# D times x: from TensorE's diagonal products to GpSimd and the eviction

## The chip, the cores and the metric

The kernel runs on one core of a Trainium2 chip. The time is the device time of one execution in microseconds (us); the time before is the median of three runs. The profile comes from one further execution.

## The reference

A state-space block and an attention block work on the same x (2048 rows, 1024 columns) and are mixed by a gate for each row.

```python
g = sigmoid((x * gate_w).sum(-1, keepdims=True))
# state space: h_t = Lam_bar * h_{t-1} + B_bar x_t, complex, 1024 states
y = 2.0 * einsum("blp,dp->bld", hseq, Cmat).real + x * Dskip
# attention: 32 heads of 32, softmax(q k / sqrt(32)) v, times wo
out = g * y + (1 - g) * b
```

All inputs and the output are bf16. The change is about the term `x * Dskip` in y: it adds, in each column, x times a number of that column.

## The kernel before

**Bursts set the beat.** Attention is cut into 512 bursts. Each has eight matmuls of scores (line 1624), two exponentials on ScalarE (ACT) from PSUM into bf16 tiles (lines 1643 and 1640, 1024 or 768 elements a partition) and products of earlier exponentials with V (line 1709) on TensorE (PE). Where an exponential has only 768 elements, the other 256 are done by VectorE (DVE) as a polynomial: line 1633 takes them from PSUM (the exponential of the same bank waits for it), lines 1667, 1668 and 1664 work on them, and GpSimd (POOL) writes the last step, x_p, in line 1665; line 1688 multiplies them with V on TensorE.

**Dense chains fill the rest.** The builder goes through the bursts one by one, calls each a period (number p, and pg = p mod 64 within one of eight head groups g), and gives each about four matmuls of 512 columns of a dense chain. All dense chains use PSUM bank 7, one after the other, and VectorE evicts the bank at the end of a chain. There are these chains: Q, K and V of the next head group (lines 1426 and 1445), u = B x (line 1457, 64 chains of eight matmuls), C chains (line 1504, 32 of them) and output chains (line 1535). An instruction's place on each engine's queue is its place in the builder's order; waits are on semaphores and worked out by `Sched`.

**State space.** A chunk of 512 rows and 128 states is an item: its u is stored to DRAM, loaded again in one piece (line 1474), rotated, scanned and rotated back on VectorE (lines 1353 and 1362). `item_ops` puts this work in a list, and the builder gives VectorE as much of it in each period as its own cost constants let it. Four chunks follow each other; GpSimd copies the last column of each (line 1365) and works out the next start (`carry`).

**A C chain** is `d_c`: 128 rows and 512 columns of y, 16 matmuls over states and real and imaginary part. Four diagonal products are put among them, each 128 by 128, with x as stationary operand and a diagonal matrix of D as moving one (lines 1508 to 1511). GpSimd builds the eight diagonals in the opening (`diag_d`, line 1306). The eviction (line 1517) multiplies by the gate into the fp32 tile Ag, of which there is one, and a DMA from SyncE's queue (SP, line 1518) stores it to DRAM; output chains load it again late in the kernel.

**Loads.** Q's weights have one slot, K's and V's two each, by head group. The builder loads K's and V's for group g + 2 at pg = 25 and Q's for g + 1 at pg = 28 (lines 1832 to 1838); Q's chains may begin at pg 32 or later, K's at any time in the group before, and all are forced when the rest of the group only just holds them. The matrix C is loaded by transposing DMAs, two for each of eight column blocks, one block every four periods from p = 28 (`C_LOADS`), and folded on VectorE afterwards. Output weights take over the places of weights that are no longer needed (`wo3`).

Of the kernel before, what the change touches and what calls it, by code (L numbers as in the profile page):

```python
# [922 lines left out]
GROUPS = 8  # L923
# [35 lines left out]
class FastPath:  # L959

    def __init__(self, nc, S, es, d, flag):
# [11 lines left out]
        wb = T("wb", [128, 8192], BF)  # L973
        self.wq = wb[:, 0:1024].rearrange("p (a n) -> p a n", a=8)
        self.wkv = wb[:, 1024:5120].rearrange("p (s q a n) -> p s q a n", s=2, q=2, a=8)
        self.bT = wb[:, 5120:8192].rearrange("p (s a n) -> p s a n", s=3, a=8)

        row = lambda o, n: wb[:, o:o + 1024 * n].rearrange("p (a n) -> p a n", a=n)
        self.wo3 = [row(1024, 2), row(5120, 3), row(3072, 1), self.cT[0][:, 0:1, :], self.cT[0][:, 1:2, :]]
        self.wo = [(self.wo3[0][:, a, :], "wo0") for a in range(2)] + [(self.wo3[4][:, 0, :], "wo4")] + [(self.wo3[1][:, a, :], "wo1") for a in range(3)]  # L980
# [6 lines left out]
        self.hpx = wb[:, 5120:8192].rearrange("p (k n) -> p k n", k=6)  # L987
# [15 lines left out]
        self.gcol = T("gcol", [128, 2, 16], F32)  # L1003
        self.ident = T("ident", [128, 128], BF)
        self.ones = self.xp[:, 0:128]
        self.diagD = T("diagD", [128, 8, 128], BF)
        self.init = T("init", [128, 2, 8], F32)
        self.hl = T("hl", [128, 2, 8], F32)
        self.cm = T("cm", [128, 4, 8], F32)
# [53 lines left out]
                     [], [("xr", r + k) for k in range(n // 128)], "ld_x", eng)  # L1063

    def w_of(self, g, part):
        return (self.wkv[:, g % 2, part - 1], ("w", g % 2, part)) if part else (self.wq, ("w", 0, 0))

    def ld_w(self, g, part, eng="sp"):
        cb = 1024 * part + 128 * g
# [83 lines left out]
    def opening(self):  # L1153
# [10 lines left out]
        for word in self.OPENING.split():  # L1164
# [9 lines left out]
            elif op in ("Ka", "Qa"):  # L1174
                self.half256(int(op == "Ka"), i, 0)
            elif op == "Kb":
                self.half256(1, i, 1)
                evac(self.K[:, 0, 256 * i:256 * (i + 1)], 7, ("K", 0, i // 2), i % 2 == 0)
            elif op == "Qb":
                self.half256(0, i, 1)  # L1180
                evac(self.Q[:, i // 2, 256 * (i % 2):256 * (i % 2 + 1)], 7, ("Q", i // 2), i % 2 == 0)
                self.spare(0.5)
            elif op in ("Va", "Vb"):
                bank, h, kt = 6, int(op == "Vb"), 2 * i + int(op == "Vb")

# [12 lines left out]
            elif op == "G":  # L1198
                g = self.gcol
                self.act(lambda e: e.activation(g[:, 0, :], g[:, 0, :], ACT.Exp, scale=-1.0), [("g0", i) for i in range(8)], ["g0"])  # L1200
                dve(lambda e: e.tensor_scalar(g[:, 0, :], g[:, 0, :], 1.0, None, ALU.add), ["g0"], ["g0"])
                dve(lambda e: e.reciprocal(g[:, 0, :], g[:, 0, :]), ["g0"], ["g0"])
                dve(lambda e: e.tensor_scalar(g[:, 1, :], g[:, 0, :], -1.0, 1.0, ALU.mult, ALU.add), ["g0"], ["g1"])
            elif op == "B":
                self.burst(8 * U + i)()
                while self.later and self.later[0][0] <= self.p:
                    self.later.pop(0)[1]()
                self.p += 1
            elif op == "M":
                S.op("pe", lambda e: e.matmul(ps[:, 6, 0:40], self.prow, self.ident[0:40, 0:40], start=True, stop=True),  # L1210
                     reads=[("prm", i) for i in range(5)] + ["ident", ("ht", 0)], writes=[("bank", 6)], name="prm")
                dve(lambda e: e.tensor_copy(self.pf[:, 0:5, :], ps[:, 6, 0:40].rearrange("p (a b) -> p a b", a=5)), [("bank", 6)],
                    [("pf", i) for i in range(5)], "prm")
# [3 lines left out]
                self.diag_d()  # L1217

    def spare(self, us):
        while self.nmath and us > 0:  # L1220
# [80 lines left out]
        ts(B2, P(FR), -2.0, ALU.mult, q(FR))  # L1301
        return ops

    def diag_d(self):
        for j in range(8):
            self.pool(lambda e, j=j: e.tensor_scalar(self.diagD[:, j, :], self.ident[:], self.pf[:, 3, j:j + 1], 0.0, ALU.mult, ALU.add),
                      ["ident", ("pf", 3)], [("diagD", j)])

    def fold_ops(self, j):

# [185 lines left out]
    def d_c(self, ch, tq, cb, k):  # L1496
# [8 lines left out]
                            tok[:1] + [("cTf", ri, j, cb)]))  # L1505


        for q in range(4):
            dt = 4 * cb + q
            mms.insert(5 * q + 3, (0, lambda e, f, l, q=q, dt=dt: e.matmul(ps[:, 7, 128 * q:128 * (q + 1)], xT[:, dt, 128 * tt:128 * (tt + 1)], self.diagD[:, dt, :],  # L1510
                                                                          start=False, stop=False), [("diagD", dt)] + self.xtok(ch)))
        a = self.Ag
        at = "Ag"
        tile = 2 * tt + cb

        def evac():
            self.dve(lambda e: e.tensor_scalar(a, ps[:, 7, :], self.gcol[:, 0, tt:tt + 1], None, ALU.mult), [("bank", 7), "g0"], [at], "evac_c")
            self.dma(lambda e: e.dma_start(self.agd[tile], a), [at], [("agd", tile)], "st_a")
            self.c_left[ch] -= 1
            self.c_end = self.p  # L1520
        return self.chain(mms, "c", evac)

    def ld_a(self, k):

# [209 lines left out]
    def build(self):  # L1734
# [7 lines left out]
        self.begin()  # L1742
        for m in range(3):
            self.ld_b(m)
        for part in (1, 2):
            self.ld_w(1, part)
        self.plan()
        self.pt_own = {}
        self.x_of, self.x_batch, self.x_when = {}, [], {}
# [40 lines left out]
        for p in range(first, NBURST):  # L1790
# [40 lines left out]

            if pg == 25 and g + 2 < GROUPS:
                assert g or not (proj[0] or cur and cur.tag == "proj")
                for part in (1, 2):
                    self.ld_w(g + 2, part)
            if pg == 28 and g + 1 < GROUPS:
                assert not (cur and cur.tag == "proj")
                self.ld_w(g + 1, 0)
            wsv = self.d["B_wo"].rearrange("(a p) n -> p a n", p=128)
            if p == 386:  # L1840
                self.dma(lambda e: e.dma_start(self.wo3[0], wsv[:, 0:2, :]), [], ["wo0"] + [("w", 0, q) for q in (1, 2)], "ld_wo")
            if not cs and cur is None and not wo1 and self.c_left[3] == 0:
                wo1 = True
                self.dma(lambda e: e.dma_start(self.wo3[1], wsv[:, 3:6, :]), [], ["wo1"] + [("bT", r) for r in range(3)] + [("hp", 8, k) for k in range(6)], "ld_wo")
            if g >= 6 and not wo6 and not cs and self.c_left[3] == 0:
                wo6 = True
                self.dma(lambda e: e.dma_start(self.wo3[3], wsv[:, 6:7, :]), [], ["wo3", ("cT", 0, 0), ("cTf", 0, 0, 0), ("cTf", 0, 0, 1)], "ld_wo")
                self.dma(lambda e: e.dma_start(self.wo3[4], wsv[:, 2:3, :]), [], ["wo4", ("cT", 0, 1), ("cTf", 0, 1, 0), ("cTf", 0, 1, 1)], "ld_wo")
            if g >= 6 and not last and not proj[7] and not us and not cs and cur is None and not self.bg:

                last = True
                xs = [("xr", r) for r in range(16)]
                assert wo1 and wo6
                self.dma(lambda e: e.dma_start(self.wo3[2], wsv[:, 7:8, :]), [], ["wo2"] + [("w", 1, q) for q in (1, 2)] + xs, "ld_wo")
# [6 lines left out]
            while used < quota:  # L1861
                if cur is None:
# [4 lines left out]
                    elif not last:  # L1867
# [268 lines left out]
```

## Time and profile before

| what | us |
|---|---|
| median of the three runs | 928.48 (926.41 to 932.98) |
| profiled execution, its own time | 928.11 |
| its span in the profile | 926.3 |
| ACT busy | 907.3 |
| TensorE busy | 902.5 |
| VectorE busy | 758.4 |
| GpSimd busy | 86.8 |

Busy time of TensorE is modelled and counts overlapping matmuls once; a busy ACT or TensorE may still be the one that waits for the other, so the page alone does not tell which of the two sets the pace. In rows of the timeline stand start, length, engine, line, operation, output and inputs, count, and in brackets the idle time before with what ended it. `SPq` marks DMA instructions in SyncE's queue.

### The profile page before, as it was taken

What the parts mean: (1) busy time and instruction counts of PE and PEld (TensorE: products, weight loads), DVE (VectorE), ACT (ScalarE), POOL (GpSimd) and SP (SyncE); (2) the same over time, 40 slices, a digit from 0 to 9 for tenths busy, and PEclk for the clock granted to TensorE, in tenths of its full rate; (3) what the DMA queues carried; (4) which work ended last, traced back from release to release, by engine and by line L of the source; (5) the groups of instructions that cost most, each with busy time, mean ns of one, the idle gap of its engine ahead of it and who ended that gap; (6) DMA issues with size and microseconds to landing.
All of it is one profiled execution on the core that took longest, in us unless ns stands there. A gap on an engine that the chain in (4) does not pass through costs nothing.

```text
span 926.3 us, 33979 instructions
## 1 busy us (share of the span) xinstructions
PE 902.5 (97%) x15316; PEld 503.9 (54%) x15316; DVE 758.4 (82%) x1310; ACT 907.3 (98%) x1034; POOL 86.8 (9%) x156
## 2 busy tenths in 40 slices
PE   8899999999999999999999999999999999999996
PEld 4554754557555565546655565555655655445553
DVE  2788989998989999989989999899988655776665
ACT  6999999999999999999999999999999999999996
POOL 2000000111000101011111020000010010001010
PEclk9999999999999999999999999999999999999998
DMA  9569747750457101272012511413001112424312
GB/s 195 87 116 184 93 84 138 144 116 5 81 113 152 50 20 49 67 147 53 19 51 65 126 45 31 104 63 103 20 15 43 31 51 77 156 83 128 114 62 75
DMA packets 170934, 77.69 MB, mean 84 GB/s; under 512 B 147232, under 2 KB 155424, under 8 KB 170784
## 3 DMA queue, kind: packets, MB, share of 16 engines
q1 hardware_dynamic: 168624, 74.94, 36.3%
q8 instruction: 121, 1.98, 0.9%
q10 hardware_dynamic: 2160, 0.53, 0.3%
q14 instruction: 29, 0.24, 0.1%
HBM read 25.18 MB, written 20.97 MB: 50 GB/s over the span
## 4 chain that ended last, share of the span: by engine, by line
PE 52%; ACT 40%; DVE 4%; DMA 2%; SPq 1%; issue 1%; POOL 0%; DVEq 0%; ACTq 0%
ACT f_pt L1643 32%; PE f_ps L1709 14%; PE f_ps L1624 10%; PE f_ps L1426 9%; PE f_ps L1504 7%; PE f_ps L1457 6%; ACT f_pt L1640 5%; PE f_ps L1445 5%; SPq L1062 1%; ACT f_cT L1643 1%; PE f_ps L1688 1%; DMA f_xT<-in_A_x_dram 1%; ACT f_Et L1643 1%; DMA f_wb<-in_A_B_im_dram 1%; DMA f_ub<-u_scratch 0%
## 5 line engine op out<-in xcount | busy, mean ns | idle before, releaser
L1643 ACT ACTIVATE f_pt<-f_ps 128x1024 bf16<-128x1024 f32 x760 | 728.8, 1090 | 1.5 <-PE f_ps L1624 1.3
L1709 PEld LDWEIGHTS f_ps<-f_V,f_pt 128*128 128x128 bf16 x7184 | 222.2, 96 | 95.3 <-issue 68.7
L1709 PE MATMUL f_ps<-f_V,f_pt 128*128 128x33 bf16 x7184 | 258.0, 178 | 0.0
L1624 PE MATMUL f_ps<-f_Q,f_K 32*128 32x256 bf16 x4096 | 203.3, 273 | 10.8 <-ACT f_pt L1643 3.3
L1640 ACT ACTIVATE f_pt<-f_ps 128x768 bf16<-128x768 f32 x184 | 165.3, 898 | 0.7 <-PE f_ps L1624 0.6
L1624 PEld LDWEIGHTS f_ps<-f_Q,f_K 32*128 32x128 bf16 x4096 | 60.7, 92 | 148.0 <-ACT f_pt L1643 120.6
L1457 PE MATMUL f_ps<-f_xT,f_wb 128*128 128x512 bf16 x512 | 131.5, 379 | 1.6 <-DMA f_wb<-in_A_B_im_dram 0.7
L1665 POOL TENSOR_SCALAR f_xp<-f_xq 128x512 int16<-128x512 f32 x92 | 67.3, 732 | 646.0 <-DVE f_xq L1664 471.3
L1426 PE MATMUL f_ps<-f_xT,f_wb 128*128 128x512 bf16 x464 | 119.3, 379 | 0.1
L1633 DVE TENSOR_SCALAR f_xi<-f_ps 128x256 int32<-128x256 f32 x184 | 77.4, 421 | 17.6 <-PE f_ps L1624 13.3
L1362 DVE TENSOR_TENSOR_SCAN f_ht<-f_pf,f_init,f_ut 128x512 bf16<-128x512 f32 x64 | 81.3, 1279 | 0.0
L1504 PE MATMUL f_ps<-f_cT,f_hp 128*128 128x512 bf16 x272 | 74.5, 379 | 0.1
L1667 DVE SCALAR_TENSOR_TENSOR f_xq<-f_xi 128x512 f32<-128x512 uint16 x92 | 63.7, 692 | 3.2
L1668 DVE SCALAR_TENSOR_TENSOR f_xq<-f_xq,f_xi 128x512 f32<-128x512 f32 x92 | 63.6, 692 | 3.1
L1664 DVE SCALAR_TENSOR_TENSOR f_xq<-f_xi,f_xq 128x512 f32<-128x512 int16 x92 | 63.5, 690 | 2.6
L1457 PEld LDWEIGHTS f_ps<-f_xT,f_wb 128*128 128x128 bf16 x512 | 40.1, 96 | 40.5 <-issue 8.6
L1535 PE MATMUL f_ps<-f_wb,f_OT 128*128 128x512 bf16 x188 | 61.2, 381 | 0.4 <-DVE f_Et L1547 0.4
L1445 PE MATMUL f_ps<-f_wb,f_xT 128*128 128x128 bf16 x896 | 59.3, 219 | 0.0
L1426 PEld LDWEIGHTS f_ps<-f_xT,f_wb 128*128 128x128 bf16 x464 | 36.1, 96 | 35.6 <-issue 7.6
L1461 DVE CAST f_ub<-f_ps 128x512 bf16<-128x512 f32 x64 | 44.1, 688 | 10.4 <-PE f_ps L1457 9.7
L1445 PEld LDWEIGHTS f_ps<-f_wb,f_xT 128*128 128x128 bf16 x896 | 50.4, 97 | 3.8 <-issue 3.8
L1722 DVE RECIPROCAL f_rc<-f_ps 128x8 f32<-128x8 f32 x63 | 13.1, 207 | 47.6 <-PE f_ps L1688 43.5
(149 smaller groups left out, 822.5 us busy)
## 6 DMA issues: line engine op xcount, KB each, us to landing
u_scratch<-f_ub SPq DMA_DIRECT2D x64, 128.0 KB, 2.1
f_ub<-u_scratch SPq DMA_DIRECT2D x32, 256.0 KB, 3.0
ag_scratch<-f_Ag SPq DMA_DIRECT2D x32, 256.0 KB, 2.0
f_hp<-ag_scratch SPq DMA_DIRECT2D x32, 256.0 KB, 3.0
f_wb<-in_B_wqkv_dram SPq DMA_DIRECT2D x21, 256.0 KB, 4.1
out_dram<-f_xT SPq DMA_DIRECT2D x16, 256.0 KB, 2.2
f_OT<-f_On SPq DMA_TRANSPOSE x63, 2.3
f_wb<-in_B_wo_dram SPq DMA_DIRECT2D x1, 768.0 KB
```

Of the source, the lines that this page charges most:

```text
L1362: ops.append((1.24, lambda ri=ri: dve(lambda e: e.tensor_tensor_scan(ht[:, ri, :], rr, ut[:, ri, :], self.init[:, ri, j:j + 1], ALU.mult, ...
L1426: mms.append((1, lambda e, f, l, a=a, w=w: e.matmul(ps[:, bank, :], w[:, a, :], xT[:, a, 512 * ch:512 * (ch + 1)], start=f, stop=l), [tok] ...
L1445: m = e.matmul(ps[:, bank, 128 * q:128 * (q + 1)], xT[:, a, 128 * kt:128 * (kt + 1)], w[:, a, :], start=(a == 0), stop=(a == 7))
L1457: mms.append((1, lambda e, f, l, a=a: e.matmul(ps[:, 7, :], bT[:, (2 * n + ri) % 3, a, :], xT[:, a, 512 * ch:512 * (ch + 1)], start=f, sto ...
L1504: mms.append((1, lambda e, f, l, j=j, ri=ri, h=h: e.matmul(ps[:, 7, :], h[:, cols], cT[ri][:, j, 512 * cb:512 * (cb + 1)], start=f, stop=l ...
L1624: m = e.matmul(ps[:, 2 * sl[h // 2] + h % 2, 256 * kl:256 * (kl + 1)], K[32 * h:32 * h + 32, g % 2, 128 * kt:128 * (kt + 1)], Q[32 * h:32 ...
L1633: first = self.dve(lambda e: e.tensor_scalar(self.xi[:, b % 2, X_COLS * n:X_COLS * (n + 1)], ps[:, 2 * s + 1, 512 - X_COLS:512], X_A, X_LO ...
L1640: self.S.op("act", lambda e: e.activation(flat(self.tile[p]), flat(ps[:, 2 * s:2 * s + 2, :]), ACT.Exp, scale=SCALE), reads=[("S", s)], wr ...
L1643: self.act(lambda e: e.activation(self.tile[p], ps[:, 2 * s:2 * s + 2, :], ACT.Exp, scale=SCALE), [("S", s)], [("pt", p)], "exp")
L1665: self.pool(lambda e: e.tensor_scalar(bits, xq[:], X_K, 128.0 * (E0 + 126.0), ALU.mult, ALU.add), ["xq"], p2, "x_p")
L1667: return [(0.73, 0.0, lambda: self.dve(lambda e: e.scalar_tensor_tensor(xq[:], lo, E2 / E3 * w, lo, ALU.add, ALU.mult), i2, ["xq"], "x_q") ...
L1709: m = e.matmul(ps[:, 6, o:o + 33], self.tile[p][:, h2, 256 * kl + 128 * qt:256 * kl + 128 * (qt + 1)], V[:, g % 2, 2 * i + kl, h, :], star ...
```

## The change

The diagonals, their tile and the four products a chain go. D is loaded as a row, broadcast to all partitions (`Dbc`), and for each C chain the matching 128 by 512 tile of x is loaded as it is stored (`xn`). When a C chain starts, GpSimd multiplies the two into Ag and scales Ag by the gate; the eviction becomes one instruction, bank times gate plus Ag. There is one `xn`; the load for the next C chain is issued two periods after a chain starts.

```diff
-        self.diagD = T("diagD", [128, 8, 128], BF)
+        self.Dbc = T("Dbc", [128, 1024], BF)
+        self.xn = T("xn", [128, 512], BF)
...
+    def ld_skip(self, tile):
+        tt, cb = divmod(tile, 2)
+        self.dma(lambda e: e.dma_start(self.xn[:], self.x2[128 * tt:128 * (tt + 1), 512 * cb:512 * (cb + 1)]), [], ["xn"], "ld_xn")
+
+    def skip(self, tile):
+        tt, cb = divmod(tile, 2)
+        self.pool(lambda e: e.tensor_tensor(self.Ag, self.xn[:], self.Dbc[:, 512 * cb:512 * (cb + 1)], ALU.mult), ["xn", "Dbc"], ["Ag"], "skip")
+        self.pool(lambda e: e.tensor_scalar(self.Ag, self.Ag, self.gcol[:, 0, tt:tt + 1], 0.0, ALU.mult, ALU.add), ["g0"], ["Ag"], "skip")
...
-            self.dve(lambda e: e.tensor_scalar(a, ps[:, 7, :], self.gcol[:, 0, tt:tt + 1], None, ALU.mult), [("bank", 7), "g0"], [at], "evac_c")
+            self.dve(lambda e: e.scalar_tensor_tensor(a, ps[:, 7, :], self.gcol[:, 0, tt:tt + 1], a, ALU.mult, ALU.add), [("bank", 7), "g0"], [at], "evac_c")
...
+            if p == C_LOADS + 34:
+                self.dma(lambda e: e.dma_start(self.Dbc[:], self.d["A_Dskip"].unsqueeze(0).to_broadcast([128, 1024])), [], ["Dbc"], "ld_D")
+                self.ld_skip(cs[0][1].tile)
...
                             cur = cs.pop(0)[1]
+                            self.skip(cur.tile)
+                            if cs:
+                                self.later.append((p + 2, lambda t=cs[0][1].tile: self.ld_skip(t)))
```

The loads move. `C_LOADS` becomes 36. K's weights have one slot instead of two and are loaded at pg = 0 of the group before theirs (for group 1 at period 17, no longer in the opening), Q's at pg = 38; V's stay. K's chains may begin at pg = 4, Q's at pg = 42.

```diff
-C_LOADS = 28
+C_LOADS = 36
+W_AT = (38, 0, 17)
...
-                proj[g][8 + c].after = max(16 * c, 32)
+                proj[g][c].after = W_AT[1] + 4
+                proj[g][8 + c].after = max(16 * c, W_AT[0] + 4)
...
-                for part in (1, 2):
-                    self.ld_w(g + 2, part)
-            if pg == 28 and g + 1 < GROUPS:
-                assert not (cur and cur.tag == "proj")
+                self.ld_w(g + 2, 2)
+            if pg == W_AT[1 if g else 2] and g + 1 < GROUPS:
+                self.ld_w(g + 1, 1)
+            if pg == W_AT[0] and g + 1 < GROUPS:
+                assert not proj[0]
                 self.ld_w(g + 1, 0)
```

The weight tile shrinks by 1024 columns, and the output weights' rows are laid out anew: row 1 moves from the weight tile, where it was loaded at period 386, to a place in C's tile beside row 2, loaded after the last C chain.

More of the change, by code (lines that the diff above doesn't have):

```diff
@@ L972, in __init__ @@
         self.V = T("V", [128, 2, 16, 4, 33], BF)
[L973 to L976, printed above, removed]
+        wb = T("wb", [128, 7168], BF)
+        self.wq, self.wk = (wb[:, 1024 * k:1024 * (k + 1)].rearrange("p (a n) -> p a n", a=8) for k in range(2))
+        self.wv = wb[:, 2048:4096].rearrange("p (s a n) -> p s a n", s=2, a=8)
+        self.bT = wb[:, 4096:7168].rearrange("p (s a n) -> p s a n", s=3, a=8)
         row = lambda o, n: wb[:, o:o + 1024 * n].rearrange("p (a n) -> p a n", a=n)
-        self.wo3 = [row(1024, 2), row(5120, 3), row(3072, 1), self.cT[0][:, 0:1, :], self.cT[0][:, 1:2, :]]
-        self.wo = [(self.wo3[0][:, a, :], "wo0") for a in range(2)] + [(self.wo3[4][:, 0, :], "wo4")] + [(self.wo3[1][:, a, :], "wo1") for a in range(3)]
+        self.wo3 = [row(2048, 1), row(4096, 3), row(3072, 1), self.cT[0][:, 0:1, :], self.cT[0][:, 1:3, :]]
+        self.wo = [(self.wo3[0][:, 0, :], "wo0")] + [(self.wo3[4][:, a, :], "wo4") for a in range(2)] + [(self.wo3[1][:, a, :], "wo1") for a in range(3)]
         self.wo += [(self.wo3[3][:, 0, :], "wo3"), (self.wo3[2][:, 0, :], "wo2")]
@@ L1065, in w_of @@
     def w_of(self, g, part):
-        return (self.wkv[:, g % 2, part - 1], ("w", g % 2, part)) if part else (self.wq, ("w", 0, 0))
+        return [(self.wq, ("w", 0, 0)), (self.wk, ("w", 0, 1)), (self.wv[:, g % 2], ("w", g % 2, 2))][part]
     def ld_w(self, g, part, eng="sp"):
@@ L1302, in math @@
         return ops
[L1304 to L1307, printed above, removed]
+    def ld_skip(self, tile):
[5 more added lines that the diff above has]
+        self.pool(lambda e: e.tensor_scalar(self.Ag, self.Ag, self.gcol[:, 0, tt:tt + 1], 0.0, ALU.mult, ALU.add), ["g0"], ["Ag"], "skip")
     def fold_ops(self, j):
@@ L1505, in d_c @@
                             tok[:1] + [("cTf", ri, j, cb)]))
[L1508 to L1511, printed above, removed]
         a = self.Ag
@@ L1520, in evac @@
             self.c_end = self.p
-        return self.chain(mms, "c", evac)
+        dn = self.chain(mms, "c", evac)
+        dn.tile = tile
+        return dn
     def ld_a(self, k):
@@ L1744, in build @@
             self.ld_b(m)
-        for part in (1, 2):
-            self.ld_w(1, part)
+        self.ld_w(1, 2)
         self.plan()
@@ L1840, in build @@
             if p == 386:
-                self.dma(lambda e: e.dma_start(self.wo3[0], wsv[:, 0:2, :]), [], ["wo0"] + [("w", 0, q) for q in (1, 2)], "ld_wo")
+                self.dma(lambda e: e.dma_start(self.wo3[0], wsv[:, 0:1, :]), [], ["wo0", ("w", 0, 2)], "ld_wo")
             if not cs and cur is None and not wo1 and self.c_left[3] == 0:
@@ L1853, in build @@
                 assert wo1 and wo6
-                self.dma(lambda e: e.dma_start(self.wo3[2], wsv[:, 7:8, :]), [], ["wo2"] + [("w", 1, q) for q in (1, 2)] + xs, "ld_wo")
+                self.dma(lambda e: e.dma_start(self.wo3[2], wsv[:, 7:8, :]), [], ["wo2", ("w", 1, 2)] + xs, "ld_wo")
             if g >= 6 and not cs and self.c_left[3] == 0 and nal < 8 and p > self.c_end:
```

7 lines of the change are left out of this document (3 added, 4 removed).

## The prediction

> **What bounds the kernel now.** I read the page first, then compared a stretch of C chains with a stretch of u chains in a table of windows, then one chain in the timeline, then what VectorE waits for in those stretches.
>
> ```profile
> span 926.3 us, 33979 instructions
> PE 902.5 (97%) x15316; PEld 503.9 (54%) x15316; DVE 758.4 (82%) x1310; ACT 907.3 (98%) x1034; POOL 86.8 (9%) x156
> ```
>
> TensorE and ScalarE both look full. Which of them sets the pace of a C chain decides what the diagonal products are worth. I cut the trace at the evictions of the C chains (line 1517): stretches of 2, 6, 8, 6, 2 and 8 chains. The last row is a stretch of u chains, which have no diagonal products.
>
> ```profile
> 296.00:310.50 14.50, 14.37 (x240) 7.69 (x236) 13.62 (x23) 14.50 (x18) 1.70 (x2) 1.00 0.51 111
> 351.50:394.60 43.10, 43.09 (x721) 23.21 (x714) 39.60 (x65) 43.10 (x50) 4.21 (x6) 1.00 0.20 62
> 460.50:518.20 57.70, 57.41 (x954) 31.12 (x951) 51.84 (x85) 57.36 (x66) 5.99 (x10) 1.00 0.18 53
> 602.00:645.20 43.20, 43.18 (x723) 23.48 (x720) 40.05 (x65) 43.20 (x50) 3.66 (x5) 1.00 0.26 77
> 686.00:700.60 14.60, 14.60 (x254) 7.98 (x247) 10.50 (x20) 14.59 (x18) 1.51 (x3) 1.00 0.21 56
> 724.00:781.20 57.20, 57.20 (x959) 30.81 (x960) 32.29 (x58) 57.07 (x66) 4.94 (x8) 1.00 0.14 44
> 135.00:194.00 59.00, 58.27 (x926) 29.27 (x925) 53.16 (x84) 58.90 (x68) 5.13 (x8) 1.00 0.78 149
> ```
>
> The columns are length, PE, PEld, DVE, ACT and POOL busy with counts, clock, DMA share and GB/s. ACT does 66 exponentials in 57.7 us of C chains (0.874 us each) and 68 in 59.0 us of u chains (0.868). ACT has no idle time in either: 57.36 of 57.70 and 58.90 of 59.00. So the C chains with their extra products run at ACT's pace, as the u chains do. VectorE is the second engine: 90 to 94% busy in the first four stretches, 72% and 56% in the last two.
>
> ```profile
> 296.76 0.69 DVE L1353 TENSOR_TENSOR f_ht<-f_ub,f_Et 128x1024 bf16<-128x1024 bf16 x1
> ...
> 296.93 1.00 POOL L1665 TENSOR_SCALAR f_xp<-f_xq 128x512 int16<-128x512 f32 x1 [15.61 <-DVE f_xq L1664]
> ...
> 297.37 1.10 DVE L1353 TENSOR_TENSOR f_tq<-f_ub,f_Et 128x1024 bf16<-128x1024 bf16 x1
> ...
> 298.72 0.22 PE L1510 MATMUL f_ps<-f_diagD,f_xT 128*128 128x128 bf16 x1
> ...
> 298.78 0.38 PE L1504 MATMUL f_ps<-f_cT,f_hp 128*128 128x512 bf16 x1
> 299.09 0.12 PEld L1624 LDWEIGHTS f_ps<-f_Q,f_K 32*128 32x128 bf16 x8 [0.26 <-ACT f_pt L1643]
> ...
> 299.71 0.42 DVE L1633 TENSOR_SCALAR f_xi<-f_ps 128x256 int32<-128x256 f32 x1
> ...
> 300.51 0.90 ACT L1640 ACTIVATE f_pt<-f_ps 128x768 bf16<-128x768 f32 x1
> ...
> 302.62 0.75 DVE L1517 TENSOR_SCALAR f_Ag<-f_ps,f_gcol 128x512 f32<-128x512 f32 x1 [0.27 <-PE f_ps L1504]
> ...
> 303.60 0.57 SPq L1518 DMA_DIRECT2D ag_scratch<-f_Ag  x1
> ...
> 309.72 0.74 DVE L1517 TENSOR_SCALAR f_Ag<-f_ps,f_gcol 128x512 f32<-128x512 f32 x1
> ```
>
> Three things are to be seen. A diagonal product takes 0.06 us of the array (298.72 to the next matmul at 298.78), and in the same period TensorE then waits 0.26 us for ACT. From one eviction to the next are 7.1 us, four periods of 1.78. And GpSimd and VectorE stop each other: the GpSimd instruction at 296.93 took 1.00 us, and the VectorE product at 297.37, whose equal ran 0.69 us just before, took 1.10.
>
> **The change part by part.**
>
> *Removed: 128 diagonal products and their weight loads.*
>
> ```profile
> L1510 PE MATMUL f_ps<-f_diagD,f_xT 128*128 128x128 bf16 x128 | 28.0, 218 | 0.0
> L1547 DVE SCALAR_TENSOR_TENSOR f_xT<-f_ps,f_gcol,f_hp 128x512 bf16<-128x512 f32 x24 | 18.0, 751 | 15.1 <-PE f_ps L1535 14.6
> L1306 POOL TENSOR_SCALAR f_diagD<-f_ident,f_pf 128x128 bf16<-128x128 bf16 x8 | 2.8, 375 | 8.6 <-DVE f_pf L1212 8.6
> L1396 POOL TENSOR_TENSOR f_cm<-f_hl,f_W 128x8 f32<-128x8 f32 x12 | 4.0, 362 | 0.2
> ```
>
> The 28.0 us are overlapped durations; the array gives up 128 x 0.06 = 7.7 us. All of it lies beside ACT, so I take 0. If TensorE set the pace it would be -7.7. The eight GpSimd instructions that built the diagonals (2.8 us) fall in the opening, beside everything: 0.
>
> *Eviction.* It becomes an instruction with a second, fp32 input from SBUF. The nearest row is line 1547 of the same shape, 751 ns against the 0.74 and 0.75 us of the evictions above: 0.
>
> *Added on GpSimd: 32 products and 32 scalings.* The scaling (512 fp32, one input, pointer scalar) is nearest to line 1665: 1.00 us with VectorE in its way, 0.62 alone (the least and the median of 92 in its own row further down). No row shows a product of two 512-wide tiles. From below it is the same 0.62; from above I let the part that grows with size double: 375 ns at 128 and 620 at 512 elements give 0.64 ns an element and 0.29 us fixed, so 0.29 + 512 x 1.28 = 0.94. I take 0.94, since line 1396 shows no product cheaper than a scaling (362 ns for only 8 elements).
>
> GpSimd itself has room. Ag is free when its store has landed (issue at 303.60, 2.0 us to landing), the product then ends near 306.6 and the scaling near 307.6; the next eviction starts at 309.72. Two microseconds are left, and x's tile is loaded a chain earlier.
>
> ```profile
> L1665 POOL TENSOR_SCALAR f_xp<-f_xq x92: 617/618/1590, 140.9 to 909.1; 128x512 int16<-128x512 f32 x92
> ...
>   PEld f_ps L1688: 0.4, 1
> ```
>
> In GpSimd's queue the skip now waits for that store, and x_p, the copies for the carry and the carry stand behind it. TensorE waits for x_p in its queue; so far this cost 0.4 us, once. An x_p that meets the pair comes up to 1.6 us later. I count 0 for it, since one wait in 92 says that x_p is nearly always early; 1 us in all is my upper bound.
>
> *The price: VectorE held up.* In the rows above a GpSimd scaling delayed a product of VectorE by 1.10 - 0.69 = 0.41 us. A GpSimd product of 0.94 instead of 0.62 us would hold it 0.41 + 0.32 = 0.73. Together 1.14 us a chain, if VectorE's next instruction has two inputs in SBUF. Those that have not, in the stretch of 351.5 to 394.6:
>
> ```profile
> L1517 DVE TENSOR_SCALAR f_Ag<-f_ps,f_gcol 128x512 f32<-128x512 f32 x6 | 4.5, 749 | 1.0 <-PE f_ps L1504 1.0
> L1633 DVE TENSOR_SCALAR f_xi<-f_ps 128x256 int32<-128x256 f32 x7 | 2.9, 418 | 0.6 <-PE f_ps L1624 0.5
> ...
> L1723 DVE SCALAR_TENSOR_TENSOR f_On<-f_ps,f_rc 128x256 bf16<-128x256 f32 x3 | 1.3, 424 | 0.1
> ...
> L1433 DVE CAST f_Q<-f_ps 128x512 bf16<-128x512 f32 x1 | 0.7, 684 | 0.0
> ```
>
> That is 9.4 of 39.6 us, about a quarter, so 0.75 of the time counts: 0.75 x 1.14 = 0.86 us a chain. Lower end 0.75 x 0.82 = 0.62 (both like line 1665), upper end 1.14; none at all if the pair fell into idle time.
>
> By the Trainium skill (SBUF — State Buffer, the section on the ports of each engine) a GpSimd instruction and a VectorE one with two SBUF inputs exclude each other for their whole length, "the other fully blocks". The 1.00 and 1.10 us above agree with that. The skill's page GPSIMD Engine Reference (section Performance versus the Vector engine) has 4497 ns for a product of 2048 fp32 elements; a quarter, as an estimate, is 1.12 us, by which the delay would be 0.75 x 1.32 = 0.99 us and the sum below about 3 us longer.
>
> What absorbs it is VectorE's own waiting. In the stretch of eight:
>
> ```profile
> DVE f_rc L1722 <- PE f_ps L1688: 2.3, 3, 1.1
> DVE f_xi L1633 <- PE f_ps L1624: 1.5, 2, 1.3
> DVE f_Ag L1517 <- PE f_ps L1504: 1.2, 3, 0.7
> ```
>
> 5.0 of its 5.86 idle microseconds are waits for TensorE, which a late VectorE can use: 0.85. The idle time of the others is 0.9, 3.5, 3.15, 4.1 and 24.9 us. So, delay less 0.85 of the idle time: 2 chains 1.7 - 0.75 = 1.0; six 5.2 - 3.0 = 2.2; eight 6.9 - 5.0 = 1.9; six 5.2 - 2.7 = 2.5; the last two stretches absorb all. Sum 7.6. In each of the four, VectorE may lag a little before ACT notices: line 1633 ended at 300.13 and the exponential that waits for it began at 300.51, so 0.4 each, 1.6 in all. **Cost 6.0 us**; at 0.62 a chain 2.8 - 1.6 with the terms floored at zero, near 1; at 1.14 12 us.
>
> *Moved: weights and C loads.*
>
> ```profile
> 66.79 1.30 SPq L1081 DMA_TRANSPOSE f_cT<-in_A_C_im_dram  x1
> ...
> 68.14 1.28 SPq L1071 DMA_DIRECT2D f_wb<-in_B_wqkv_dram  x1
> ...
> 73.34 0.69 DVE L1353 TENSOR_TENSOR f_ht<-f_ub,f_Et 128x1024 bf16<-128x1024 bf16 x1 [2.39 <-DMA f_ub<-u_scratch]
> ...
> 77.36 1.94 ACT L1643 ACTIVATE f_OT<-f_ps 128x1024 bf16<-128x1024 f32 x2 [1.34 <-PE f_ps L1624]
> ```
>
> Here the load of u that VectorE waits for comes behind a C load and Q's weights in SP's queue and lands late; VectorE, then TensorE, then ACT stop, 1.34 us. The C loads go from period 28 to 36 and Q's weights to 38, past this u load: -1.3. At the other end two C loads and K's weights now meet the loads of B for later u chains; by the same row that costs 0 to 1.3. K's weights come at a group's start; the chains that use them may begin four periods (7.1 us) later and begin later still, against 4.1 us to land.
>
> ```profile
> f_wb<-in_B_wqkv_dram SPq DMA_DIRECT2D x21, 256.0 KB, 4.1
> u_scratch<-f_ub SPq DMA_DIRECT2D x64, 128.0 KB, 2.1
> ```
>
> The 32 loads of x (128 KB, like the second row) are hidden by their chain of lead; each holds SP until the product before has read its tile, with u loads and stores behind it, a few tenths at most. D's row is read long before its use. I take -1.0 for the whole part, ends -1.3 and +1.3.
>
> Sum: 926.3 and 1.8 us around it are 928.1 for this execution, which is the median of the three runs within 0.4. 928.1 + 6.0 - 1.0 = **933 us**.
>
> **The rivals.**
>
> *Covered.* The pair falls into VectorE's waits and evictions, and the early stall goes: 928.1 - 1.3 = 926.8, not slower. For it: GpSimd's instructions now start at a DMA's landing, not behind a VectorE product. Against: the waits are one place in seven.
>
> *TensorE set the pace.* 928.1 - 7.7 = 920.4. For it: 97% busy. Against: the 0.26 us wait for ACT and the equal pace of u chains.
>
> *Nothing is absorbed.* VectorE's waits return because TensorE is late with it, and the product's hold is the upper end: 22 chains x 1.14 - 1.6 = 23.5; with half of the idle time used, 5.7, 17.8: 946 us. It decides where a chain's delay exceeds what it can use, 0.5 to 0.6 us. For it: stretches over 90% busy; ACT waits directly for line 1633.
>
> *GpSimd late for the eviction.* If the pair took more than 4 us the eviction would wait, TensorE behind it. Four waits of 0.26 us a chain give 1 us back; at 6 us each of the 26 chains that follow another loses 1: 954.
>
> **How the numbers follow.** Forecast 0.56, covered 0.22, TensorE's pace 0.02, nothing absorbed 0.16, GpSimd late 0.04. The forecast alone spans 928 to 940. The range 925.5 to 944 holds covered, the forecast, and nothing absorbed where a little more than half of the idle time is used. One per cent, about what a measurement here can tell from no change, is 919.2 and 937.8: slower by more has the last two rivals and a tenth of the forecast, 0.26; faster 0.02; same 0.72.
>
> **What would show it.** Right: ACT idle or stretched intervals inside the first four C stretches, with waits of ACT or TensorE on VectorE there and none in the last eight chains; VectorE products near 1.1 or 1.4 us beside GpSimd; the wait at 77 us gone. Wrong: C stretches as long as before (covered), shorter by 0.06 us a product (TensorE), or the eviction waiting for GpSimd.

## The result and the profile after

| | before | after |
|---|---|---|
| median of 6 runs, us | 929.15 (926.41 to 932.98) | 954.21 (951.95 to 955.33) |
| ratio to before (95%) | | 1.0267 (1.0239 to 1.0294) |
| profiled execution, us | 928.11 | 952.96 |

The time before is here the median of the three runs above and three more. The change costs 25.1 us, five times the 5 us forecast, and the time lies outside the range, beyond 944. The two profiled executions differ by 24.9 us of span, so the traces can be set side by side. The page of after, its span and its first lines:

```profile
span 951.2 us, 33831 instructions
...
PE 903.0 (95%) x15188; PEld 494.0 (52%) x15188; DVE 775.9 (82%) x1310; ACT 908.9 (96%) x1034; POOL 158.5 (17%) x212
```

ACT has the same work as before (907.3 us then) in a longer span: ACT now stands still. The six stretches of C chains, 2, 6, 8, 6, 2 and 8 of them, cut at the evictions as in the prediction (columns as there: length, PE, PEld, DVE, ACT, POOL busy with counts, clock, DMA share, GB/s):

```profile
296.50:311.20 14.70, 14.44 (x238) 7.09 (x236) 13.66 (x22) 14.66 (x18) 3.66 (x4) 1.00 0.31 91
354.40:403.30 48.90, 45.14 (x726) 22.32 (x725) 44.40 (x67) 45.89 (x52) 17.86 (x17) 1.00 0.27 81
469.70:537.60 67.90, 56.63 (x848) 27.33 (x845) 54.44 (x81) 54.74 (x62) 22.22 (x23) 0.92 0.23 70
622.50:673.00 50.50, 43.56 (x674) 21.47 (x674) 44.09 (x66) 43.59 (x50) 16.66 (x15) 0.97 0.24 73
711.50:726.00 14.50, 14.44 (x248) 7.49 (x247) 11.82 (x20) 14.50 (x18) 6.07 (x7) 1.00 0.23 61
749.10:806.30 57.20, 57.02 (x950) 28.85 (x947) 33.08 (x60) 57.20 (x67) 19.67 (x23) 1.00 0.19 60
```

Length less ACT's busy time is 0.04, 3.01, 13.16, 6.91, 0 and 0 us, 23.1 in all; in the six rows of before it was 0.5. So 22.6 of the 24.9 us are ACT idle in stretches two to four, and the last two stretches lose nothing. What ACT and TensorE wait for, in the waits of the whole span (engine, output and line, releaser: us in total, times, longest):

```profile
ACT f_pt L1646 <- PE f_ps L1627: 21.6, 21, 4.7
...
PEld f_ps L1691 <- POOL f_xp L1668: 12.1, 4, 4.4
PE f_ps L1691 <- POOL f_xp L1668: 11.7, 4, 4.3
...
PE f_ps L1509 <- DVE f_Ag L1518: 7.7, 9, 1.4
...
ACT f_pt L1643 <- DVE f_xi L1636: 4.0, 6, 0.8
```

ACT waits for TensorE, and TensorE for two things: x_p from GpSimd (12.1 us in 4 waits, where before had 0.4 in one), and bank 7 from the eviction (7.7 us in 9 waits). The longest of the four in the timeline (in brackets the idle time before and what ended it):

```profile
472.09 0.72 DVE L1518 SCALAR_TENSOR_TENSOR f_Ag<-f_ps,f_gcol,f_Ag 128x512 f32<-128x512 f32 x1
...
472.84 0.32 SPq L1519 DMA_DIRECT2D ag_scratch<-f_Ag  x1
473.06 0.68 DVE L1667 SCALAR_TENSOR_TENSOR f_xq<-f_xi,f_xq 128x512 f32<-128x512 int16 x1
...
476.17 1.15 POOL L1311 TENSOR_TENSOR f_Ag<-f_xn,f_Dbc 128x512 f32<-128x512 bf16 x1 [3.75 <-DMA ag_scratch<-f_Ag]
...
477.42 0.69 POOL L1312 TENSOR_SCALAR f_Ag<-f_Ag,f_gcol 128x512 f32<-128x512 f32 x1
...
478.20 0.62 POOL L1668 TENSOR_SCALAR f_xp<-f_xq 128x512 int16<-128x512 f32 x1
...
478.87 0.27 PE L1691 MATMUL f_ps<-f_V,f_xp 128*128 128x33 bf16 x4 [4.32 <-POOL f_xp L1668]
...
481.07 1.02 ACT L1646 ACTIVATE f_pt<-f_ps 128x1024 bf16<-128x1024 f32 x1 [4.74 <-PE f_ps L1627]
```

The input of x_p was ready at 473.74 (473.06 + 0.68). GpSimd was idle but took x_p only at 478.20. At the head of its queue stood the product, which waits for the store of Ag: issued at 472.84, landed by 476.17, 3.3 us. Then the pair ran, 2.0 us, and x_p came behind it. TensorE stood 4.3 us in its queue for x_p, and ACT 4.7 us for TensorE's next scores. The trace of before told which x_p cannot afford this. Its rows for x_p and for the matmul that takes it:

```profile
380.96 1.00 POOL L1665 TENSOR_SCALAR f_xp<-f_xq 128x512 int16<-128x512 f32 x1 [5.75 <-DVE f_xq L1664]
...
385.51 0.26 PE L1688 MATMUL f_ps<-f_V,f_xp 128*128 128x33 bf16 x4
...
469.23 0.99 POOL L1665 TENSOR_SCALAR f_xp<-f_xq 128x512 int16<-128x512 f32 x1 [1.41 <-DVE f_xq L1664]
470.29 0.27 PE L1688 MATMUL f_ps<-f_V,f_xp 128*128 128x33 bf16 x4 [0.27 <-POOL f_xp L1665]
...
483.71 0.62 POOL L1665 TENSOR_SCALAR f_xp<-f_xq 128x512 int16<-128x512 f32 x1 [8.18 <-DVE f_xq L1664]
484.38 0.27 PE L1688 MATMUL f_ps<-f_V,f_xp 128*128 128x33 bf16 x4
...
610.66 0.62 POOL L1665 TENSOR_SCALAR f_xp<-f_xq 128x512 int16<-128x512 f32 x1 [8.23 <-DVE f_xq L1664]
611.33 0.27 PE L1688 MATMUL f_ps<-f_V,f_xp 128*128 128x33 bf16 x4
```

They are the 27th, 37th, 39th and 51st of the 92 instructions that write x_p. The first is typical: 3.6 us lie between the end of x_p and its use (the median of all 92 is 3.7). The second is the one wait that before had: TensorE already stood for it, 0.27 us. At the last two the matmul starts 0.05 us after x_p ends, so there was no time to spare either. The same four are the four waits of after, and the last three of them are its large stops. ACT's rows at the second and third of these stops:

```profile
500.61 1.94 ACT L1646 ACTIVATE f_pt<-f_ps 128x1024 bf16<-128x1024 f32 x2 [4.00 <-PE f_ps L1627]
...
635.81 2.98 ACT L1646 ACTIVATE f_pt<-f_ps 128x1024 bf16<-128x1024 f32 x3 [3.98 <-PE f_ps L1627]
```

ACT's three waits are 4.74, 4.00 and 3.98 us, 12.7 together. The fourth late x_p is the typical one of the rows above. In after GpSimd stood 4.93 us ahead of it, until the store had landed, and the pair then took 2.7 us:

```profile
389.61 0.62 POOL L1668 TENSOR_SCALAR f_xp<-f_xq 128x512 int16<-128x512 f32 x1
```

TensorE stood 1.23 us for it and ACT then 1.02. So 3.6 us to spare were not enough either.

The pair itself, as after's trace has it (least, median and longest duration in ns, first and last start):

```profile
L1311 POOL TENSOR_TENSOR f_Ag<-f_xn,f_Dbc x32: 1149/1158/1577, 281.8 to 801.0; 128x512 f32<-128x512 bf16 x32
L1312 POOL TENSOR_SCALAR f_Ag<-f_Ag,f_gcol x32: 692/1004/1536, 283.0 to 802.5; 128x512 f32<-128x512 f32 x32
L1518 DVE SCALAR_TENSOR_TENSOR f_Ag<-f_ps,f_gcol,f_Ag x32: 717/748/753, 303.2 to 805.3; 128x512 f32<-128x512 f32 x32
```

The product takes 1.15 us undisturbed and the scaling 0.69, 1.84 where the prediction had 1.56. The eviction with its second input costs no more than the old one. What the pair does to VectorE is seen in the timeline of after, where the same VectorE instruction (line 1670) stands once without the pair and once beside it:

```profile
354.60 0.69 DVE L1670 SCALAR_TENSOR_TENSOR f_xq<-f_xi 128x512 f32<-128x512 uint16 x1
...
363.80 1.48 POOL L1311 TENSOR_TENSOR f_Ag<-f_xn,f_Dbc 128x512 f32<-128x512 bf16 x1 [5.98 <-DMA ag_scratch<-f_Ag]
...
364.81 1.02 DVE L1670 SCALAR_TENSOR_TENSOR f_xq<-f_xi 128x512 f32<-128x512 uint16 x1
```

It takes 1.02 us in place of 0.69. The product took 1.48 in place of 1.15: a VectorE product with two inputs (line 1358) was running from 363.58 to 364.27 when it began. Each holds up the other.

### The profile page after: what moved, and what is told of

Read it like the earlier page. It is cut to its first block, busy times and chain, and to the rows that moved or that the text cites. A ratio compares the mean times of both kernels' runs of the same rounds, so it can differ in the third digit from the quotient of the medians.

```text
span 951.2 us, 33831 instructions
## 1 busy us (share of the span) xinstructions
PE 903.0 (95%) x15188; PEld 494.0 (52%) x15188; DVE 775.9 (82%) x1310; ACT 908.9 (96%) x1034; POOL 158.5 (17%) x212
## 4 chain that ended last, share of the span: by engine, by line
PE 51%; ACT 29%; DVE 12%; issue 2%; DMA 2%; POOL 1%; SPq 1%; DVEq 0%; ACTq 0%
ACT f_pt L1646 24%; PE f_ps L1712 13%; PE f_ps L1627 10%; PE f_ps L1431 9%; PE f_ps L1509 6%; PE f_ps L1462 6%; PE f_ps L1450 5%; ACT f_pt L1643 4%; DVE f_ut L1358 2%; DVE f_Ag L1518 1%; DVE f_tq L1358 1%; DMA ag_scratch<-f_Ag 1%; DVE f_ht L1367 1%; SPq L1064 1%; ACT f_cT L1646 1%
## 5 line engine op out<-in xcount | busy, mean ns | idle before, releaser
L1367 DVE TENSOR_TENSOR_SCAN f_ht<-f_pf,f_init,f_ut 128x512 bf16<-128x512 f32 x64 | 83.5, 1314 | 0.0
L1509 PE MATMUL f_ps<-f_cT,f_hp 128*128 128x512 bf16 x272 | 71.4, 382 | 5.1 <-DVE f_Ag L1518 4.1
L1311 POOL TENSOR_TENSOR f_Ag<-f_xn,f_Dbc 128x512 f32<-128x512 bf16 x32 | 40.4, 1263 | 123.3 <-DMA ag_scratch<-f_Ag 122.8
L1538 PE MATMUL f_ps<-f_wb,f_OT 128*128 128x512 bf16 x156 | 54.3, 382 | 0.4 <-DVE f_Et L1550 0.4
L1466 DVE CAST f_ub<-f_ps 128x512 bf16<-128x512 f32 x64 | 44.0, 688 | 11.6 <-PE f_ps L1462 8.9
```

The source lines that it names most:

```text
L1367: ops.append((1.24, lambda ri=ri: dve(lambda e: e.tensor_tensor_scan(ht[:, ri, :], rr, ut[:, ri, :], self.init[:, ri, j:j + 1], ALU.mult, ...
L1509: mms.append((1, lambda e, f, l, j=j, ri=ri, h=h: e.matmul(ps[:, 7, :], h[:, cols], cT[ri][:, j, 512 * cb:512 * (cb + 1)], start=f, stop=l ...
```

## The experiments

The theory from the traces had two parts: the place of the pair in GpSimd's queue makes x_p late (about 15 us was expected of it), and the pair holds VectorE, which makes evictions and x_in late (line 1636, which takes the polynomial's input from PSUM before ACT may begin on the same bank). Rivals were that the moved loads cost the time, that the new tile or eviction costs it, or that GpSimd's mere activity does. All ratios are to the kernel before on the same chip.

**The loads alone.** After, with the diagonals, their four products a chain and the old eviction put back and the pair, D's row and the tile of x taken out:

```diff
-                            self.skip(cur.tile)
+            mms.insert(5 * q + 3, (0, lambda e, f, l, q=q, dt=dt: e.matmul(..., xT[:, dt, ...], self.diagD[:, dt, :], ...)))
```

> The moved loads and K's single slot alone; diagonal products, their eviction and the diagonals stay as before. Theory 'queue' (x_p stands behind the skip pair in GpSimd's queue, the pair waits for Ag's store) and theory 'lock' (the pair holds VectorE off) both expect the time of before within 3 us, 926 to 932: the 1.46 us stop at 75 us goes, one of 1.7 us near 142 us comes. Theory 'loads' (a good part of the 25 us comes from the moved loads) expects 935 or more.

Measured: 928.06 us, 0.9989 (0.9976 to 1.0003). The moved loads are worth between -2.2 and +0.3 us; they are not the cause.

**The pair two periods later.** The same work on the same engine, put into the queues two periods after the chain starts, behind the x_p that is due:

```diff
-                            self.skip(cur.tile)
+                            self.later.append((p + 2, lambda t=cur.tile: self.skip(t)))
```

> After, with one thing changed: the pair on GpSimd is issued two periods after its C chain starts and not at its start, so an x_p of the first two periods stands ahead of it in the queue. Same instructions, same port use. Theory 'queue': the stops of 4.9, 4.1 and 4.1 us with the short ones behind them go, 15 us less, 939 to 942. Theory 'lock': the pair holds VectorE as long as before, 952 to 955.

Measured: 937.65 us, 1.0090 (1.0062 to 1.0118). One line of order gives back 16.6 of the 25.1 us, a little more than expected. Its waits:

```profile
PE f_ps L1509 <- DVE f_Ag L1518: 11.6, 13, 1.6
...
ACT f_pt L1646 <- PE f_ps L1627: 6.5, 15, 1.0
...
ACT f_pt L1643 <- DVE f_xi L1636: 4.8, 7, 0.8
...
PE f_ps L1691 <- POOL f_xp L1668: 0.3, 1, 0.3
```

TensorE's wait for x_p has gone from 11.7 to 0.3 us. What stays are ACT's waits, 6.5 and 4.8 us, 11.3 in all; behind the first of them I read TensorE's wait for bank 7.

**No pair.** The pair is left out, so D times x is missing from the result; Ag is cleared once at the start, and the loads, the tile of x and the new eviction stay.

```diff
-                            self.skip(cur.tile)
+                            pass
```

> After without the two GpSimd instructions of each C chain (D times x is left out of the output; the loads of x, the eviction with two inputs and the moved loads stay; Ag is set once in the opening). Both theories, queue and lock, expect all of the loss to go: 926 to 930, since ACT sets the pace and TensorE's saving of 7.7 us lies beside it. If TensorE set the pace of the C chains: 921. If the eviction or the loads of x cost something: above 932.

Measured: 925.87 us, 0.9968 (0.9953 to 0.9983). So the late pair costs 11.8 us, and everything else of the change together is a small gain. Where the 11.8 go is seen in the first four stretches, cut at the same evictions (7 us ahead of the first to 1 us behind the last). Without the pair:

```profile
294.90:309.90 15.00, 14.43 (x242) 7.29 (x240) 13.95 (x23) 15.00 (x18) 1.70 (x2) 1.00 0.39 95
350.60:394.00 43.40, 41.94 (x691) 21.16 (x701) 40.06 (x66) 43.40 (x50) 4.21 (x6) 1.00 0.29 86
459.40:516.60 57.20, 55.20 (x901) 28.18 (x913) 51.63 (x85) 57.04 (x65) 6.05 (x10) 1.00 0.26 78
600.50:643.50 43.00, 41.69 (x688) 21.36 (x696) 39.95 (x65) 43.00 (x50) 3.78 (x5) 1.00 0.27 83
```

With the late pair:

```profile
295.30:311.20 15.90, 14.47 (x242) 7.30 (x240) 15.60 (x23) 15.90 (x19) 7.11 (x6) 1.00 0.35 90
351.80:397.50 45.70, 41.30 (x684) 21.11 (x690) 44.31 (x65) 44.73 (x51) 20.42 (x18) 1.00 0.31 81
462.50:525.30 62.80, 55.24 (x912) 29.01 (x926) 59.61 (x85) 58.70 (x66) 26.70 (x26) 1.00 0.26 75
609.00:656.90 47.90, 42.57 (x682) 21.82 (x688) 44.64 (x65) 43.97 (x50) 19.69 (x17) 0.96 0.25 75
```

VectorE has nearly the same instructions (239 and 238) and is busy 1.65, 4.25, 7.98 and 4.69 us longer, 18.6 for 22 chains or 0.84 a chain. The stretches are 0.9, 2.3, 5.6 and 4.9 us longer, 13.7 in all (a little more than the 11.8 of the medians). Of VectorE's 13.0 idle microseconds without the pair only 4.9 were used, 37%. The last two stretches, where VectorE has most room, take as long with the late pair as without (6.93 and 48.65 us from first to last eviction, against 6.92 and 48.65): there all of the hold is absorbed.

**The pair into a tile of its own.** At the original place, but the pair writes a new bf16 tile xs that the eviction adds, so that it waits for the eviction before it and not for the store of Ag:

```diff
-        self.pool(lambda e: e.tensor_tensor(self.Ag, self.xn[:], ...), ["xn", "Dbc"], ["Ag"], "skip")
-        self.pool(lambda e: e.tensor_scalar(self.Ag, self.Ag, ...), ["g0"], ["Ag"], "skip")
+        self.pool(lambda e: e.tensor_tensor(self.xs[:], self.xn[:], ...), ["xn", "Dbc"], ["xs"], "skip")
+        self.pool(lambda e: e.tensor_scalar(self.xs[:], self.xs[:], ...), ["g0"], ["xs"], "skip")
```

> After, with the pair writing to a bf16 tile of its own, which the eviction adds; the pair then waits for the eviction before and not for the store behind it, some 3.3 us less. Still issued at the chain's start. Queue: an x_p that is due early waits for a pair of 2 us at most and not for store and pair: the three stops shrink from 4 to 5 us to about 1 us, 942 to 946. Lock alone: no less than 951.

Measured: 943.67 us, 1.0152 (1.0121 to 1.0183). Its wait of TensorE for x_p:

```profile
PE f_ps L1692 <- POOL f_xp L1669: 4.6, 3, 1.9
```

Three waits stay, now 1.9 us at most, the length of a pair, where they were up to 4.3. So taking the wait for the store off the head of the queue gives back 10.5 us, and the kernel is still 6.0 us longer than with the late pair. How these 6.0 split is not shown: part is the pair ahead of x_p, part may be VectorE, which its page has busy 787.6 us, against 775.9 in after and 777.6 with the late pair.

**Writing without reading.** At the late place the pair is replaced by three memsets of Ag (512, 512 and 256 columns); D times x is missing here too.

```diff
-        self.pool(lambda e: e.tensor_tensor(self.Ag, self.xn[:], ...), ["xn", "Dbc"], ["Ag"], "skip")
-        self.pool(lambda e: e.tensor_scalar(self.Ag, self.Ag, ...), ["g0"], ["Ag"], "skip")
+        for n in (512, 512, 256):
+            self.pool(lambda e, n=n: e.memset(self.Ag[:, 0:n], 0.0), [], ["Ag"], "skip")
```

> The kernel with the late pair, but the two GpSimd instructions of a chain are replaced by three that only write Ag (memsets of 512, 512 and 256 columns; D times x is left out). A memset of 512 took 0.78 us in the run without the pair, so the three take about 2 us, as long as the pair, in the same places and with the same waits. If VectorE is held because GpSimd reads SBUF (lock on reads): the 11.8 us between the late pair (937.65) and no pair (925.87) go, 925 to 928. If any GpSimd instruction of that length holds VectorE, or if the wait for Ag itself costs it: 935 to 938.

Measured: 926.03 us, 0.9968 (0.9951 to 0.9984), against 925.87 without anything there. The pages of the kernel without the pair, and then of this one:

```profile
PE 879.1 (95%) x14967; PEld 492.0 (53%) x15188; DVE 758.2 (82%) x1310; ACT 905.8 (98%) x1034; POOL 85.0 (9%) x149
```

```profile
PE 898.5 (97%) x15188; PEld 492.1 (53%) x15188; DVE 757.8 (82%) x1310; ACT 905.9 (98%) x1034; POOL 128.1 (14%) x244
```

VectorE is busy 757.8 us, as without the pair; with the late pair it was 777.6. From first to last eviction each of the six stretches takes what it takes without the pair, within 0.01 us. The memsets were shorter than expected, 0.53, 0.53 and 0.31 us in this trace, 1.36 a chain where the undisturbed pair takes 1.84. So neither the waits around Ag nor GpSimd's being busy for 1.36 us costs anything. What the memsets lack is an input that is read from SBUF; that it is the reading, and not the missing 0.5 us, the next version bears out.

**The product alone.** At the late place without the scaling, so the added term lacks the gate.

```diff
-        self.pool(lambda e: e.tensor_scalar(self.Ag, self.Ag, self.gcol[:, 0, tt:tt + 1], 0.0, ALU.mult, ALU.add), ["g0"], ["Ag"], "skip")
```

> The late pair without its second instruction (the scaling by the gate is left out). If the 11.8 us are the sum of two holds, of about 1.0 us for the product and 0.5 for the scaling, and VectorE absorbs about 0.5 us a chain: 931 to 933. If they came from waiting for the pair as a whole (store, product, scaling in a row, late for the eviction): 926 to 928, as the pair then ends 0.7 to 1.5 us earlier.

Measured: 933.40 us, 1.0052 (1.0037 to 1.0068), a little above what was expected of two holds. The product costs 7.5 of the 11.8 us and the scaling 4.3, near the ratio of their lengths, 1.15 to 0.69. The product alone is shorter than the three memsets, reads, and costs 7.5 us where they cost nothing.

**The same term on VectorE.** One instruction at the late place, x times gate times D into xs, which the eviction adds; GpSimd does nothing for it.

```diff
-        self.pool(lambda e: e.tensor_tensor(self.Ag, self.xn[:], ...), ["xn", "Dbc"], ["Ag"], "skip")
-        self.pool(lambda e: e.tensor_scalar(self.Ag, self.Ag, ...), ["g0"], ["Ag"], "skip")
+        self.dve(lambda e: e.scalar_tensor_tensor(self.xs[:], self.xn[:], self.gcol[:, 0, tt:tt + 1], self.Dbc[...], ALU.mult, ALU.mult), ["xn", "Dbc", "g0"], ["xs"], "skip")
```

> The same product and scaling as one VectorE instruction of 0.69 us at the late place, into a bf16 tile of its own; GpSimd has nothing of it. VectorE's delay per chain is then 0.69 us by itself, with no lock. By the prediction's sum of delay less what VectorE's waits absorb, 0.69 us a chain costs about 2 to 3 us over no pair: 928 to 930. If a lag of VectorE is hardly absorbed (22 chains of 0.69 less 1.6): 939.

Measured: 931.46 us, 1.0037 (1.0021 to 1.0053). Its row among the groups of its page:

```profile
L1312 DVE SCALAR_TENSOR_TENSOR f_xs<-f_xn,f_gcol,f_Dbc 128x512 bf16<-128x512 bf16 x32 | 23.7, 742 | 0.0
```

Giving VectorE the work costs 5.6 us over no pair, more than the 2 to 3 expected; giving it to GpSimd costs 11.8. The instruction takes 742 ns, but its neighbours overlap with it (one that begins at 472.50 is followed by the next at 473.16): in the first four stretches, cut in the same way, VectorE is busy 11.4 us longer than without the pair (18.6 with the late pair), and they are 6.7 us longer (13.7). So 4.7 us of VectorE's idle time are used, about as many as the hold used. The product alone fits in between: 14.4 us busier, 9.1 us longer, 5.3 used. The VectorE version is cheaper because it adds less to VectorE's busy time, not because more is absorbed.

**The loads again.** Two versions of the loads-alone kernel, to see what the stop near 143 us is, which came with the moved loads. First K's weights of group 2 twelve periods later:

```diff
-            if pg == W_AT[1 if g else 2] and g + 1 < GROUPS:
+            if pg == W_AT[1 if g else 2] + (12 if g == 1 else 0) and g + 1 < GROUPS:
```

> Loads only (diagonal products as before), with K's weights of group 2 loaded 12 periods into group 1 and not at its start, away from the last C load. If the 1.25 us stop near 143 us comes from that load meeting C's and B's, it goes: 927 against 928.06 of loads only. If C's last loads alone make B's late, the stop stays: 928.

Measured: 926.21 us, 0.9974 (0.9960 to 0.9989). The stop stayed (1.0 us), so this load isn't its cause; the time cannot be told from that of the loads alone. Then the C loads four periods earlier, halfway back:

```diff
-C_LOADS = 36
+C_LOADS = 32
```

> Loads only (diagonal products as before), with the C loads from period 32 and not 36. If the stop of ACT near 143 us (1.2 us in loads only) comes from C's last load meeting the loads of B and of Q's and K's weights, it goes, since C's last block then comes four periods earlier: 926.5 to 927.5. If it comes from K's weights and the u chains alone, it stays, 928. The stop at 75 us stays away in both, since Q's weights are out of its way; if it comes back, it was the C loads that made it.

Measured: 925.84 us, 0.9952 (0.9938 to 0.9966), lower than before by 4.4 us on its chip: the lowest ratio of all versions that compute the whole result, and it keeps the diagonal products. The stretch around 143 us, in the loads alone and then in this version:

```profile
136.00:147.00 11.00, 8.83 (x155) 4.66 (x159) 9.00 (x13) 9.79 (x12) 0.62 (x1) 1.00 1.09 192
```

```profile
136.00:147.00 11.00, 10.69 (x165) 5.05 (x162) 9.56 (x16) 10.90 (x13) 0.62 (x1) 1.00 0.80 167
```

ACT is idle 1.2 us with the C loads from period 36 and 0.1 from period 32, with the DMA share falling from 1.09 to 0.80; ACT's wait at 77 us is gone as well. What TensorE waits for at the stop is a load of B for the u chains: 1.6 us in the loads alone, not at all in this version. So the place of the C loads makes the stop, as the prediction's term for the other end had it. The stop is in every version with the C loads from period 36, 1.0 to 1.8 us of ACT's time, and once more: the profiled execution with the memsets has 4.0 us there, outside the C stretches. The profiled executions' spans differ by 2.2 us (924.1 against 926.3); the other 2.1 of the 4.4 us come from before, whose median on this chip is 930.21 where its profiled execution took 928.11.

## Why the prediction was wrong

**The order in GpSimd's queue: the step that failed.** The prediction named what stands behind the pair and that TensorE waits for x_p, and then wrote "I count 0 for it, since one wait in 92 says that x_p is nearly always early; 1 us in all is my upper bound". It was 16.6 us. Two readings in it were wrong. One wait in 92 says that x_p is seldom late, not that it is early: besides the one that was late, two in the C stretches came with no more than 0.05 us to spare, and the rows of before show them. And an x_p that meets the pair was priced at "up to 1.6 us", the pair's own length; but the pair waits for a DMA at the head of an in-order queue, and all that time is x_p's too: TensorE stood 4.3 us at the longest, and even an x_p with 3.6 us to spare came late. The prediction had both numbers (store issue, 2.0 us to landing) and used them only for the pair against its own eviction. ACT's stops at the four late x_p are 13.7 us. From first to last eviction the first four stretches are 0.0, 1.0, 9.05 and 3.0 us longer than with the late pair, 13.05 in all, and the spans of the two profiled executions differ by 15.2; where the rest of the 16.6 lies is not shown.

**VectorE's hold: right in mechanism, in size partly by luck.** 0.86 us a chain was forecast; 0.84 was measured with the late pair. Two errors cancelled: the product was sized 0.94 us and took 1.15, the scaling 0.62 and took 0.69, by which the prediction's formula would give 0.75 x (0.48 + 0.94) = 1.07; so less of VectorE's time than the three quarters assumed was held. The Trainium skill (GPSIMD Engine Reference, Performance versus the Vector engine) has 4497 ns for an addition of two tiles of 2048 fp32 elements (it times no product there); a quarter of it, 1.12 us, was the prediction's estimate, and the 1.15 us of the trace agree with it. The Trainium skill also says (SBUF — State Buffer, Who interferes with whom) that a VectorE instruction with two SBUF inputs contends with a GpSimd instruction that reads SBUF and not with one that only writes it; the memsets, 926.03 us against 925.87, agree.

**Absorption: the second step that failed.** 0.85 of VectorE's idle time and 0.4 us of free lag in each stretch left 6.0 us; it was 11.8, at the upper end of 12 that the prediction gave this term. VectorE's idle time was used by 37%, and with the product alone or with the work on VectorE hardly differently: 4.7 to 5.3 of 13.0 us in all three, where the prediction took 0.85. As I read it, a wait of VectorE for TensorE is free time only if the delay falls ahead of it and nobody waits for VectorE in between: the delay falls at one place, at the pair, and soon behind it VectorE does the eviction and x_in, for which TensorE (11.6 us in 13 waits) and ACT (4.8 in 7) wait. No run moves the delay alone, so this reason is argued, and the share is what is shown. The working of this term also has slips: 0.85 was read from the stretch of eight alone (in the two of six, 2.8 of 3.5 and 2.2 of 3.15 us of VectorE's idle time are waits for TensorE); the terms of its lower end add up to 2.2 and not 2.8, which gives 0.6 us and not near 1; and half of the idle time of the first four stretches is 6.7 us, not 5.7, which puts that rival at 945 and not 946. None of them changes the outcome.

**ACT sets the pace: right.** Between the loads alone (928.06) and no pair (925.87) lie 2.2 us, of the 7.7 that the products would give if TensorE set the pace. The two also differ in the eviction and the loads of x, and their intervals overlap. The evictions of the two traces tell where the difference lies: from first to last, the last eight chains take 49.58 us with the products and 48.65 without, 0.13 us a chain of the 0.24 that four products would give; the first four stretches together take 127.57 and 127.06. So 0 was nearly right in the first four stretches and a little too strict in the last chains.

**Eviction, loads, last stretches: right.** The eviction took 748 ns. The loads were forecast at -1.0 and measured at -1.0 (-2.2 to +0.3, so the time alone doesn't tell them from nothing): the stop at 77 us went, and one near 143 us came, as the term for the other end allowed. The last ten chains lost nothing.

**The rivals.** For VectorE's part the 11.8 us lie midway between the forecast's 6.0 and the 17.8 of "nothing is absorbed" with half of the idle time used; by the share that was used, 37%, this rival was nearer. "GpSimd late for the eviction" had the right time, 954, by luck, for a mechanism that didn't occur: no eviction waits for GpSimd in the waits of after. GpSimd was late for another customer.

One after the other, the versions give: queue 16.6, hold 11.8, loads -1.0, products -2.2, together 25.2 of 25.1 us. That these add up is no proof, since each is the difference of one version to the next; and the hold is measured with the pair at the late place, not at the place where the change has it.

## What to carry to other kernels

Before work that waits for a DMA is put into an in-order queue, list what stands behind it and read for each of those, occurrence by occurrence, how long after its end its consumer starts (its slack); the count of waits in a profile says nothing of the slack. Then set the slack against the whole time at the head of the queue, the wait for the DMA included, and not against the length of the new work. Moving work off an engine that doesn't set the pace gained little here (2.2 us of 7.7), and moving it to GpSimd beside a VectorE that is 90% busy in that stretch costs VectorE part of GpSimd's time, here 0.84 us a chain for a pair of 1.84; in this kernel VectorE doing the work itself was cheaper by half. If the work must go there, put it behind the short instruction that is due, and let it wait for something that comes early.

## What the runs showed of the hardware

Not expected: after a stop of 4 us TensorE comes back slower. Three stretches of after's table of windows, ahead of the largest stop, in it and behind it:

```profile
470.00:474.50 4.50, 4.47 (x76) 2.24 (x74) 4.31 (x7) 4.50 (x7) 0.19 (x1) 1.00 0.19 58
474.60:478.80 4.20, 0.00 (x0) 0.00 (x0) 0.00 (x0) 1.74 (x2) 2.44 (x3) 1.00 0.29 65
478.90:482.50 3.60, 3.60 (x41) 1.56 (x42) 3.01 (x7) 1.43 (x2) 0.00 (x0) 0.57 0.12 27
```

TensorE had nothing for 4.2 us, and for the 3.6 us after that its granted clock was 0.57. By the Trainium skill (TensorE: Matmul & The Clock Gate, What's actually happening) an idle window of about 3.4 us drops the array to half of its clock; the trace agrees. How much this adds to a stop was not measured. And GpSimd's memsets of the fp32 tile Ag (0.53 us for 512 columns) leave VectorE's busy time where it was, 757.8 us against 758.2, while the scaling of the same tile (0.69 us) behind the product makes it longer, from 772.7 us with the product alone to 777.6.
